# Reordering the first chunk of a fused mLSTM cell and feed-forward block by hand

## The chip, the core and the metric

The kernel runs on one core of a Trainium2 chip. The metric is the device time of one execution in microseconds (us), as the median of several executions. The core has five engines with an instruction queue each, in order: TensorE (PE in the profile, with its weight loads PEld), VectorE (DVE), ScalarE (ACT), GpSimd (POOL) and SyncE (SP, which here only issues DMAs).

## The reference

The first half is an mLSTM cell over 4 batches, 8 heads, 768 tokens and 40 dimensions per head: a decaying outer-product state that each token updates and reads. The second half is a feed-forward block over the 3072 resulting rows of 320 values.

```python
for t in range(S):
    m_new = np.maximum(f_gate[:, :, t] + m, i_gate[:, :, t])
    f_stab = np.exp(f_gate[:, :, t] + m - m_new)
    i_stab = np.exp(i_gate[:, :, t] - m_new)
    C = f_stab[...] * C + i_stab[...] * np.einsum('bhd,bhe->bhde', vt, kt)
    n = f_stab[...] * n + i_stab[...] * kt
    h_tilde = np.einsum('bhde,bhe->bhd', C, qt)
    denom = np.maximum(np.abs(np.einsum('bhd,bhd->bh', n, qt)[:, :, None]), 1.0)
    y[:, :, t] = sigmoid(o_gate[:, :, t]) * h_tilde / denom
...
h = x @ w_in                      # 3072x320 by 320x2048
out = np.maximum(0.01 * h, h) @ w_out
```

## The kernel before

**Tiling.** The 768 tokens are cut into 6 chunks of 128. In each chunk there is one step per batch, so steps 0 to 3 are chunk 0, steps 4 to 7 chunk 1, and so on. A cell step turns 128 tokens of 8 heads into one block of x, and the four blocks of a chunk, transposed, are the 512 columns (`xT`) of the feed-forward block for that chunk. The feed-forward block of chunk c runs on TensorE between the cell steps of chunk c+1.

**Chunk 0** is the subject here. It has no earlier state, so a step works on plain scores:

- `gates` (scans on VectorE, L293 to L312) and `gates_exp` (ScalarE, L318 to L324) make the decay factors. `gates_T` (called by `u_gates(1)` for chunk 1) transposes them with TensorE (L341, L346) and copies them out with VectorE (L354, L356).
- `spread_first` builds the decay exponents of two steps in four PSUM banks with TensorE (L460 to L477); `first_exp` (ScalarE, L488) takes their exponential into the weights `w`.
- `u_transpose` transposes k and q of a step (TensorE L598, tile `tkq`), and a copy (L601, on VectorE for step 0, on ScalarE for the others) gives `kqT`.
- `u_scores` multiplies them (TensorE L610), and VectorE multiplies the scores into `w` (L614).
- `u_natural` transposes k back (TensorE L620, ScalarE copy L622); `prep_vu` scales v for the state (POOL, L513 and L517); `u_state` multiplies both (TensorE L631, `dC`) and copies the state (ScalarE L639).
- `u_values` multiplies `w` by v (TensorE L700, `pa`) and makes the reciprocal denominators (VectorE L692 to L694). `prep_o` takes the tanh of the output gate (ScalarE L539); `gate` joins them (VectorE L709, then POOL L713, tile `x`).
- `u_x` transposes a block of x (TensorE L801 and L802), and five ScalarE copies (L804 to L808) put it into `xT`.
- `prepare_tiles` (POOL L153 to L156) and `prepare_step` (POOL L160 to L162) set constant parts of the tiles that the later chunks use. `prepare_step` overwrites parts of the same tile that holds v of the step.

**The weights** come as 64-bit floats. `load_weights(n)` loads a part; `narrow_weights(n)` is a generator of seven passes over it that make 32-bit floats: one on ScalarE (L254) and six on VectorE (L256, L260, L264, L266, L268, L270). In chunk 0 parts 0 and 1 of `w_in` are narrowed, in chunk 1 all the rest, while VectorE also serves the cell.

**Feed-forward units of chunk 0.** `ff_units(0)` gives units of 10 matmuls of 256 columns (L819), each with two ScalarE activations (L827). `ffs[0]` and `ffs[1]` use part 0 of `w_in` and the columns of steps 0 and 1; they run in chunk 0's own code. The others run in the loop over chunk 1, which starts with the split transposes of step 4 (`u_split`, L579, tile `tk`).

**What sets the order.** TensorE, VectorE, ScalarE and POOL run in the order in which `first_chunk` (L1144) calls these functions (`manual_schedule`, L1229). SP's DMAs are placed by a scheduler. PSUM tiles of tag "c" share four buffers, so a new tile waits until an older one has been read. Each DMA that SP issues waits for the one eight places before it to land.

Of the kernel before, what the change touches and what calls it, by code (L numbers as in the profile page):

```python
# [19 lines left out]
def kernel(  # L20
# [110 lines left out]
    for n in range(NL):  # L131
# [2 lines left out]
        nc.gpsimd.memset(S_t[n][:, 1, :, D:], 2.0)  # L134
        nc.gpsimd.memset(S_t[n][SL:, 0], 0.0)

    def mixed(s):

        n = s % 2
        return qn[:, 2 * n : 2 * n + 2]  # L140
# [9 lines left out]
    def prepare_tiles():  # L150

        for u in range(2):
            nc.gpsimd.tensor_copy(cm2[ts(u, SL)], cmask[ts(u, SL), ts(u, SL)])  # L153
        nc.gpsimd.memset(xb[:], 0.0)
        for t in rb_t:
            nc.gpsimd.memset(t[:, :, RL:], 0.0)  # L156

    def prepare_step(n):

# [48 lines left out]
    def load_weights(n):  # L208

        m = n - QN  # L210
        if n < QN:
            dst = w_in[:, n, :]
        else:
            dst = w_out[:, 2 * m : 2 * m + 2, :].rearrange("p a d -> p (a d)")
        to = dst
        if wide:
            if n < 2:
                at = NF * GT - 2 * WC * (n + 1)
                raw = acts_l[:, at : at + 2 * WC].bitcast(U64)
            elif n < QN:  # L220
                raw = raw_t[:, WC * (n - 2) : WC * (n - 1)]
            elif m < 2:
                raw = w_out[:].rearrange("p f d -> p (f d)")[:, (2 + m) * WC : (3 + m) * WC].bitcast(U64)
            else:
                at = (4, 0, 1, 2, 3, 4)[m - 2] * HW
                raw = raw_t[:, at : at + HW]
            raws[n] = (raw, dst)
            to = raw
        if n < QN:
            src = moe_w_in[:, n * QC : (n + 1) * QC].rearrange("(k p) (r c) -> r p k c", p=DP, r=2)  # L230
            at = [0, 0]
            for r in (0, 1, 0, 1):
                k0, m = run_of(r, at[r])
                nc.sync.dma_start(
                    to[DP * r : DP * (r + 1), 2 * P * at[r] : 2 * P * (at[r] + m)].rearrange("p (k c) -> p k c", k=m),
                    src[r, :, k0 : k0 + 2 * m - 1 : 2, :],
                )
                at[r] += m
        else:
            rows = moe_w_out[2 * m * P : 2 * (m + 1) * P, :]  # L240
            nc.sync.dma_start(to.rearrange("p (a d) -> p a d", d=Dm), rows.rearrange("(a p) d -> p a d", p=P))
# [118 lines left out]
    def load(s):  # L360
        c, b = divmod(s, B)
        rows = ts(c, P)
        d = st.setdefault(s, {})
        n = s % NL
        d.update(k=kn[:, n], q=qn[:, n])
        if c == 0:
            d["va"] = S_t[n][:, 1]
            for t, src in ((kn, k), (qn, q)):
                nc.sync.dma_start(  # L369
                    t[:, n].rearrange("p h d -> p (h d)")[:, : TJ * D], src[b, :, rows, :].rearrange("h (g j) d -> h g (j d)", j=TJ),  # L370
                )
            nc.sync.dma_start(d["va"][:, :, :D], v[b, :, rows, :].rearrange("h p d -> p h d"))
            return
        if s not in asked:
            load_kq(s)
        for u in range(2):
            for i in range(2):
                nc.sync.dma_start(
                    S_v[n][ts(u, SL), u, :, i, :DB],
                    v[b, :, c * P + u * SL : c * P + (u + 1) * SL, DB * i : DB * (i + 1)].rearrange("h p d -> p h d"),  # L380
                )
# [11 lines left out]
    def load_o(s):  # L393
        c, b = divmod(s, B)
        at = NF * GT - 4 * WC - (s + 1) * Dm
        st.setdefault(s, {})["o"] = acts_l[:, at : at + Dm]
        nc.sync.dma_start(
            st[s]["o"].rearrange("p (h d) -> p h d", d=D), o_gate[b, :, ts(c, P), :].rearrange("h p d -> p h d"),
        )
# [54 lines left out]
    def spread_first(a, s2):  # L454


        M = H // RG
        ab = [psf.tile([P, 2, M, P], F32, name=f"ab{r}", tag="mm") for r in range(RG)]
        for r in range(RG):
            nc.tensor.matmul(  # L460
                ab[r][:].rearrange("p n m t -> p (n m) t"), lhsT=identb, rhs=cmaskb.unsqueeze(1).to_broadcast([P, 2 * M, P]),
                start=True, stop=False,
            )
        for n in range(2):
            for m in range(M):
                for r in range(RG):
                    bh = (s2 + n) * H + m * RG + r
                    rows = ts(r, BH)
                    nc.tensor.matmul(
                        ab[r][:, n, m, :], lhsT=ident[rows, r * BH + bh : r * BH + bh + 1].to_broadcast([BH, P]),  # L470
                        rhs=a[rows, :], start=False, stop=False,
                    )
        for r in range(RG):
            rows = ts(r, BH)
            at = r * BH + s2 * H + r
            ones = ident[rows, at : at + (2 * M - 1) * RG + 1 : RG]
            nc.tensor.matmul(  # L477
                ab[r][:].rearrange("p n m t -> p (n m) t"), lhsT=i0[rows, :], rhs=ones.unsqueeze(2).to_broadcast([BH, 2 * M, P]),
                start=False, stop=True,
            )  # L480
        return ab

    def first_exp(ab, s2):

        for n in range(2):
            w = st[s2 + n]["w"] = wk.tile([P, H, P], F32, name="w", bufs=NL)
            for r in range(RG):
                nc.scalar.activation(w[:, r::RG, :], ab[r][:, n], AF.Exp)  # L488
# [47 lines left out]
    def prep_o(s):  # L536

        o = st[s]["o"] if s < B else natural(s, 2) if s < 2 * B else raw_blocks(s, 2, DB)
        nc.scalar.activation(o, o, AF.Tanh, scale=0.5)  # L539
# [63 lines left out]
    def u_scores(s):  # L603
        d = st[s]
        kqT, w = d["kqT"], d["w"]
        sc = [psc.tile([P, PR, P], F32, name=f"sc{r}", tag="c") for r in range(2)]
        for j in range(PR):
            for r in range(2):
                rows = slice(DP * r, DP * r + D)
                nc.tensor.matmul(  # L610
                    sc[r][:, j, :], lhsT=kqT[rows, 0, ts(j, P)], rhs=kqT[rows, 1, ts(j, P)], start=True, stop=True,
                )
        for r in range(2):
            nc.vector.tensor_tensor(w[:, r::2, :], w[:, r::2, :], sc[r][:], op=ALU.mult)  # L614
# [71 lines left out]
    def u_state(s):  # L686
        state(s)
        state_copy(s)
# [388 lines left out]
    def u_gates(c):  # L1077
        gates_T(c, bus.pop(c)[0])
# [65 lines left out]
    def first_chunk():  # L1144

        load_fi(1)
        load_fi(2)
        for n in range(2):
            load(n)
        load_weights(0)  # L1150
        load_o(0)
        load_o(1)
        for n in range(2, B):
            load(n)
        load_o(2)
        load_o(3)
        load_weights(1)
        gates(0)
        gates_exp(0)
        bu, a, _ = bus[0]  # L1160
        warm(9)
        ab = spread_first(a, 0)
        gates_T(0, bu)
        first_exp(ab, 0)
        gates(1)
        u_transpose(0, nc.vector.tensor_copy)
        gates_exp(1)
        u_transpose(1, nc.scalar.copy)
        prep_vu(0)
        prep_vu(1)  # L1170
        load_kq(B)
        u_scores(0)
        ab = spread_first(a, 2)
        u_scores(1)
        first_exp(ab, 2)
        u_natural(0)
        u_natural(1)
        w = narrow_weights(0)
        next(w, None)
        u_values(0)  # L1180
        u_values(1)
        next(w, None)
        next(w, None)
        prep_o(0)
        gate(0)
        prep_o(1)
        gate(1)
        prepare_tiles()
        u_x(0)
        u_x(1)  # L1190
        for _ in w:
            pass
        u_transpose(2, nc.scalar.copy)
        u_transpose(3, nc.scalar.copy)
        ffs = ff_units(0)
        ffs[0]()
        u_state(0)
        u_state(1)
        prepare_step(0)
        prepare_step(1)  # L1200
        u_scores(2)
        u_scores(3)
        prep_o(2)
        prep_o(3)
        ffs[1]()
        u_values(2)
        gate(2)
        u_values(3)
        gate(3)
        w = narrow_weights(1)  # L1210
        next(w, None)
        next(w, None)
        u_x(2)
        u_x(3)
        prep_vu(2)
        prep_vu(3)
        for _ in w:
            pass
        u_gates(1)
        u_natural(2)  # L1220
        u_state(2)
        u_natural(3)
        u_state(3)
        prepare_step(2)
        prepare_step(3)
        return ffs
# [125 lines left out]
```

## Time and profile before

| quantity | value |
|---|---|
| median of 3 runs | 510.76 us (510.48 to 511.11) |
| the profiled execution's own time | 510.94 us |
| its span (first to last instruction) | 509.1 us |
| TensorE busy (matmuls) | 495.4 us, 97% of the span |
| TensorE weight loads | 385.9 us, 76% |
| VectorE busy | 332.4 us, 65% |
| ScalarE busy | 179.3 us, 35% |
| POOL busy | 143.2 us, 28% |
| mean DMA rate | 116 GB/s |

A busy TensorE is not TensorE at its peak: the chip grants it a clock, shown as PEclk in tenths of full speed, and a matmul at half clock is busy for longer. The profile also cuts the span into 40 slices of 12.7 us with the busy tenths of each engine; the first five slices (to 63.6 us) hold chunk 0 and the start of chunk 1. A wait is named by what ended it.

### The profile page before, as it was taken

The numbers are of one execution on the slowest core, as the hardware profiler recorded it, in microseconds if no ns is written. First come the engines' busy times: TensorE is split into PE (matmuls) and PEld (weight loads), VectorE is DVE, ScalarE is ACT, GpSimd is POOL, SyncE is SP. The second block draws the span as 40 slices with busy tenths as digits, with TensorE's granted clock in tenths as the row PEclk, the third lists the DMA queues.
The fourth block names the chain that finished last, engine by engine and source line by source line (L and its number), as shares of the span: only waits on it lengthen the run. The fifth ranks groups of instructions, "written<-read, shape, count | busy, mean of one in ns | idle before, by whom it ended". The sixth has DMA issues, their size and how long they took to land.

```text
span 509.1 us, 13257 instructions
## 1 busy us (share of the span) xinstructions
PE 495.4 (97%) x5362; PEld 385.9 (76%) x5362; DVE 332.4 (65%) x543; ACT 179.3 (35%) x476; POOL 143.2 (28%) x177
## 2 busy tenths in 40 slices
PE   8788899999999999999999999999999999999997
PEld 7667688867755469965479965489955489999997
DVE  5455888899963976824976734867633767864831
ACT  4465657752552331042421133511312510035210
POOL 4063905434320501620502701403700302200011
PEclk9878699999999999999999999999999999999999
DMA  6999976597460584872685872775871211200001
GB/s 130 174 175 169 256 135 183 125 203 140 96 159 7 116 160 133 152 152 85 135 161 131 141 161 79 155 149 120 162 186 30 55 53 41 88 4 1 1 1 52
DMA packets 157556, 59.25 MB, mean 116 GB/s; under 512 B 120056, under 2 KB 148280, under 8 KB 157496
## 3 DMA queue, kind: packets, MB, share of 16 engines
q1 hardware_dynamic: 117428, 51.20, 44.7%
q10 hardware_dynamic: 40068, 7.21, 9.2%
q8 instruction: 42, 0.69, 0.6%
q14 instruction: 18, 0.15, 0.1%
HBM read 51.68 MB, written 6.70 MB: 115 GB/s over the span
## 4 chain that ended last, share of the span: by engine, by line
PE 89%; SPq 3%; DMA 3%; DVE 2%; issue 1%; POOL 1%; ACT 1%; ACTq 0%; DVEq 0%; POOLq 0%
PE ph L819 34%; PE po L897 30%; PE pq L1004 6%; PE po L854 6%; PE pT L754 3%; PE sd L673 3%; SPq L369 2%; DMA kn<-in_k_dram 1%; PE tkq L598 1%; PE sd L678 1%; DMA fi<-in_f_gate_dram 1%; PE tk L579 1%; DMA S<-in_v_dram 1%; PE pa L700 1%; POOL x L713 1%
## 5 line engine op out<-in xcount | busy, mean ns | idle before, releaser
L819 PE MATMUL ph<-xT,w_in 64*128 64x512 f32 (+1 forms) x960 | 180.7, 526 | 0.5 <-issue 0.5
L819 PEld LDWEIGHTS ph<-xT,w_in 64*128 64x128 f32 x960 | 92.4, 189 | 74.8 <-issue 68.2
L897 PEld LDWEIGHTS po<-w_out,acts 128*128 128x128 f32 x640 | 87.3, 190 | 3.4 <-issue 3.0
L897 PE MATMUL po<-w_out,acts 128*128 128x160 f32 x640 | 89.1, 300 | 0.0
L827 ACT ACTIVATE acts<-ph 128x512 f32<-128x512 f32 (+1 forms) x96 | 45.5, 522 | 121.7 <-PE ph L819 108.4
L651 POOL TENSOR_TENSOR S<-S,f 40x336 f32<-40x336 f32 x36 | 31.8, 883 | 132.6 <-PE pT L754 94.1
L683 DVE TENSOR_TENSOR qn<-w,sd 64x512 f32<-64x512 f32 x40 | 27.4, 684 | 43.8 <-PE sd L678 28.4
L503 ACT ACTIVATE w<-w,gT 128x64 f32<-128x64 f32 x160 | 41.2, 337 | 21.3 <-DMA S<-in_v_dram 15.8
L897 PE MATMUL po<-raw,acts 128*128 128x160 f32 x320 | 44.7, 300 | 0.0
L897 PEld LDWEIGHTS po<-raw,acts 128*128 128x128 f32 x320 | 43.6, 190 | 0.3
L854 PE MATMUL po<-w_out,acts 128*128 128x320 f32 x128 | 36.5, 436 | 0.0
L495 POOL TENSOR_TENSOR w<-w,i 128x512 f32<-128x512 f32 x20 | 29.0, 1458 | 25.3 <-DMA w<-a_dr 10.5
L768 POOL TENSOR_TENSOR xb<-xb,den 128x320 f32<-128x320 f32 x16 | 11.6, 727 | 76.5 <-DVE xb L765 76.5
L761 DVE STREAM_TRANSPOSE hb<-pT 128x512 f32<-128x512 f32 x16 | 11.4, 713 | 31.0 <-PE pT L754 30.8
L854 PEld LDWEIGHTS po<-w_out,acts 128*128 128x128 f32 x128 | 23.6, 190 | 9.3 <-issue 0.3
L556 DVE TENSOR_TENSOR qn<-kqT,ea 64x512 f32<-64x512 f32 x32 | 27.0, 845 | 1.0
L932 POOL TENSOR_TENSOR y<-y,raw 128x160 f32<-128x160 f32 x10 | 8.2, 819 | 64.9 <-ACT y L931 64.9
L673 PEld LDWEIGHTS sd<-kqT 40*64 40x64 f32 x640 | 19.8, 135 | 6.1 <-issue 6.1
L772 DVE STREAM_TRANSPOSE x<-xb 128x512 f32<-128x512 f32 x16 | 18.0, 1124 | 7.7 <-POOL xb L768 7.7
L897 PE MATMUL po<-raw 128*128 128x160 f32 x160 | 22.6, 299 | 0.0
L897 PEld LDWEIGHTS po<-raw 128*128 128x128 f32 x160 | 22.0, 190 | 0.0
L673 PE MATMUL sd<-kqT 40*64 40x64 f32 x640 | 21.3, 220 | 0.0
(205 smaller groups left out, 701.4 us busy)
## 6 DMA issues: line engine op xcount, KB each, us to landing
rb<-in_k_dram SPq DMA_DIRECT2D x64, 80.0 KB
rb<-in_q_dram SPq DMA_DIRECT2D x64, 80.0 KB
rb<-in_o_gate_dram SPq DMA_DIRECT2D x64, 80.0 KB
ea<-a_dr SPq DMA_DIRECT2D x32, 128.0 KB
raw<-in_moe_w_out_dram SPq DMA_DIRECT2D x6, 640.0 KB
w<-a_dr ACTq DMA_DIRECT2D x24, 128.0 KB
xT<-x_dr SPq DMA_DIRECT2D x32, 96.0 KB
x_dr<-x SPq DMA_DIRECT2D x64, 40.0 KB
```

The source lines that it names most:

```text
L495: nc.gpsimd.tensor_tensor(w, w, cm2.unsqueeze(1).to_broadcast([P, H, SL]), op=ALU.add)
L503: yield nc.scalar.activation(w[:, h, :], w[:, h, :], AF.Exp, bias=gT[c][:, 0, bh : bh + 1], scale=1.0)
L556: nc.vector.tensor_tensor(mixed(s)[rows, 1 - r], d["kqT"][rows, 1].rearrange("p (h t) -> p h t", t=SL), d["ea"][rows], op=ALU.mult,)
L651: nc.gpsimd.tensor_tensor(new, old, g, op=ALU.mult)
L673: nc.tensor.matmul(bank[1 - u][toks, h, :], lhsT=kqT[rows, 0, ts(h, SL)], rhs=kqT[rows, 1, ts(h, SL)], start=True, stop=True,)
L683: nc.vector.tensor_tensor(mixed(s)[toks, u], w[toks], bank[1 - u][toks], op=ALU.mult)
L772: nc.vector.transpose(in_blocks(xq[:]), xb[:].rearrange("p (j n) d -> p j n d", n=TB))
L819: nc.tensor.matmul(ph[r][:, cols], lhsT=w_row(r, slot, j), rhs=xT[DP * r : DP * (r + 1), slot, cols], start=(slot == 0), stop=(slot == KC ...
L827: nc.scalar.activation(acts[:, f, cols], ph[r][:, cols], AF.Prelu, alpha=0.01)
L854: nc.tensor.matmul(po[n][:], lhsT=acts[:, f, ts(n, P)], rhs=w_out[:, f, :], start=(f == 0), stop=(f == NF - 1),)
L897: nc.tensor.matmul(bank[:], lhsT=left[:, f, :], rhs=right[:, f, :], start=f == 0, stop=f == KH - 1)
L1004: nc.tensor.matmul(bank[r][:, e, :], lhsT=left(r)[rows, e], rhs=right(r)[rows], start=n == 0, stop=n == len(terms) - 1,)
```

## The change

Only `first_chunk`, the place of one group of memsets and the order of some loads change. No instruction is added or removed.

```diff
+    for t in rb_t:
+        nc.gpsimd.memset(t[:, :, RL:], 0.0)
...
         nc.gpsimd.memset(xb[:], 0.0)
-        for t in rb_t:
-            nc.gpsimd.memset(t[:, :, RL:], 0.0)
...
+        load_weights(1)
         load_o(2)
         load_o(3)
-        load_weights(1)
...
         u_scores(0)
+        u_scores(1)
         ab = spread_first(a, 2)
-        u_scores(1)
         first_exp(ab, 2)
+        u_gates(1)
         u_natural(0)
         u_natural(1)
-        w = narrow_weights(0)
-        next(w, None)
         u_values(0)
         u_values(1)
-        next(w, None)
-        next(w, None)
+        prepare_tiles()
+        prepare_step(0)
+        prepare_step(1)
+        w = narrow_weights(0)
+        for _ in range(3):
+            next(w, None)
         prep_o(0)
+        prep_o(1)
         gate(0)
-        prep_o(1)
         gate(1)
-        prepare_tiles()
+        u_transpose(2, nc.scalar.copy)
+        u_state(0)
+        u_transpose(3, nc.scalar.copy)
+        u_state(1)
         u_x(0)
         u_x(1)
+        prep_vu(2)
+        prep_vu(3)
         for _ in w:
             pass
-        u_transpose(2, nc.scalar.copy)
-        u_transpose(3, nc.scalar.copy)
         ffs = ff_units(0)
         ffs[0]()
-        u_state(0)
-        u_state(1)
-        prepare_step(0)
-        prepare_step(1)
         u_scores(2)
         u_scores(3)
         prep_o(2)
         prep_o(3)
-        ffs[1]()
         u_values(2)
-        gate(2)
         u_values(3)
-        gate(3)
         w = narrow_weights(1)
         next(w, None)
-        next(w, None)
+        ffs[1]()
+        gate(2)
+        gate(3)
         u_x(2)
         u_x(3)
-        prep_vu(2)
-        prep_vu(3)
         for _ in w:
             pass
-        u_gates(1)
         u_natural(2)
```

In words, engine by engine. **TensorE**: the scores of step 1 stand before the second `spread_first`; the gate transposes of chunk 1 move from behind the last x up to just behind that `spread_first`; the transposes of steps 2 and 3, with the state products of steps 0 and 1 between them, stand before the x transposes of steps 0 and 1 instead of behind them and behind `ffs[0]`; the values of steps 2 and 3 stand before `ffs[1]` instead of behind it. **ScalarE**: the copies of those tiles move likewise, so four `kqT` copies and two state copies come before the ten `xT` copies of steps 0 and 1; the first pass of `narrow_weights(1)` comes before the activations of `ffs[1]`. **VectorE**: the two gate copies move up; both denominators of steps 2 and 3 come before both gate products. **POOL**: the constant memsets and copies come before the products of x(0) and x(1), and the scaled v of steps 2 and 3 before the products of x(2) and x(3). **SP**: part 1 of `w_in` is asked for before the output gates of steps 2 and 3; a few loads for chunk 1 change places with neighbours.

## The prediction, made before the result was known

> **What bounds the kernel now.** I read the slices first, for where TensorE is not full and what clock it has.
>
> ```profile
> PE   8788899999999999999999999999999999999997
> ...
> PEclk9878699999999999999999999999999999999999
> ```
>
> Only the first five slices (63.6 us) have room: from there on TensorE is full at full clock, and the 448.6 us behind 60.4 hold 444.4 us of it. So the change is worth what it moves the start of the chunk 1 loop, unless the loop gives it back. Second, the chain of waits in order of time, for what fills those 60 us (start, length, what):
>
> ```profile
> 25.27 0.49 DVE x L709
> ...
> 26.51 1.98 POOL x L713
> ...
> 29.43 5.52 PE tkq L598 x128
> 34.95 2.36 PE ph L819 x20
> ...
> 42.85 3.71 PE pa L700 x32
> ...
> 47.76 1.18 POOL x L713
> ...
> 52.27 0.43 ACT kn L622
> ...
> 54.72 0.43 ACT kn L622
> ```
>
> After each pair of `pa`, TensorE waits for gate products on VectorE and POOL; the `tkq` of steps 2 and 3 stand behind that wait, and the end of the chunk is a ping-pong between TensorE and ScalarE copies. Third, stretches of 2 us, for the granted clock (columns: length, busy time of PE, PEld, DVE, ACT, POOL, then PEclk, DMA share, GB/s):
>
> ```profile
> 22.00:24.00 2.00, 1.16 (x10) 1.01 (x9) 0.73 (x4) 0.06 (x1) 0.00 (x0) 0.69 0.94 179
> 24.00:26.00 2.00, 0.00 (x0) 0.00 (x0) 1.97 (x4) 0.00 (x0) 0.17 (x1) 0.50 1.01 138
> ...
> 32.00:34.00 2.00, 2.00 (x58) 2.00 (x57) 0.21 (x1) 1.41 (x2) 1.77 (x5) 0.75 1.17 199
> 34.00:36.00 2.00, 2.00 (x44) 1.84 (x40) 0.00 (x0) 2.00 (x3) 0.02 (x1) 1.00 1.46 140
> ...
> 46.00:48.00 2.00, 1.36 (x8) 0.87 (x7) 1.51 (x6) 0.00 (x0) 0.96 (x2) 0.67 1.41 154
> ...
> 60.00:62.00 2.00, 2.00 (x20) 1.71 (x20) 1.97 (x2) 1.76 (x6) 1.92 (x3) 0.92 1.05 358
> ```
>
> Only 1.0 and 0.5 stand in undivided stretches, so the mixed means place the switches: down at about 22.8, up at 33.0, down at 46.7, up at 60.3. The distances (10.2, 13.7, 13.6) are 3, 4 and 4 times 3.41 us. Each fall comes at the end of 3.8 us of `pa`, during which PE was busy without a gap; each rise after several us of dense `tkq` or `ph`. At half clock a tile of 16 `tkq` matmuls takes 1.70 us instead of 1.05, and a `ph` unit about 4.3 instead of 2.4.
>
> [...] The sum goes by the trace.
>
> **The change, part by part**, on the trace's clock; the sum counts to the ScalarE pass L254 of `w_in` part 2, at 56.80, which opens the work of the loop (its `kqT` copies and exponentials follow without a gap).
>
> *To the end of the first values.* Scores of step 1 before `spread_first`: both are 1.1 and 3.2 us on either side, so the exchange is free; the exponentials of steps 2 and 3 slip from 17.13 to about 18.2 and the copies L622 and L254 behind them end near 22.8 instead of 21.3, still ahead of the second denominators, at 24.5, that L256 stands behind. The gate transposes took 0.46 + 0.85 at half clock, so about 0.65 at full, now in front of `pa`. `pa` ends at 23.16 + 0.65 = **23.8**, and L709 moves from 25.27 to 25.9.
>
> *The stretch to `ffs[0]`, now ScalarE's.* x is ready at 27.3 and 29.2, as before plus 0.65, but TensorE goes on with `tkq` at 23.8. ScalarE then has, in this order: four `kqT` copies (3.04 for three, so 4.05), two state copies (1.25 for four, so 1.25 for both steps), ten `xT` copies (27.54 to 29.21, 1.67 a step, 3.34). They sum to 8.64. They start after the first `tkq` tile, at 24.9. One stall comes between: the k tile of step 3 waits for the PSUM buffer of step 2's q copy and takes 1.05, of which the state copy covers 0.62, so about 0.5. `ffs[0]` starts at 24.9 + 8.64 + 0.5 = **34.05** against 34.88: **-0.83**. VectorE's narrowing ended at 32.2; plus 0.65, plus 0.4 because POOL now scales v beside it (L268 took 1.89 beside POOL's L513 and L517, 1.49 otherwise), it ends at 33.3. It is late next, by 0.75.
>
> *The clock under `ffs[0]`.* Before, TensorE reached it straight from dense `tkq`, at full clock. Now it runs dry from about 30.8 (second x transpose) to 34.05. With the switch points of before it falls at 33.0 and rises at 36.4, and of the 2.36 us at half clock half is lost: **+1.2**. The bounds are 0 (no fall) and +2.4 (no rise before 39.8).
>
> *From `ffs[0]` to the last `xT` copy.* Before it took 51.59 - 34.88 = 16.71. Now: `ffs[0]` 2.43, scores of step 2 1.07, the product L614 and its start 1.33 (step 3's pair lies under `pa`), `pa` 2 x 1.89, together 8.61; then `ffs[1]` 2.36 runs while VectorE and POOL make x (denominator 0.57, L709 0.45, L713 0.72, so 1.74: hidden); then activations 0.74 and ten `xT` copies 3.34. Sum 15.05: **-1.66**. If `ffs[1]` falls to half clock behind `pa`, up to 1.9 of it is lost.
>
> *From there to L254.* Before 5.21, with the gate transposes, the first `nk` on TensorE and 1.02 us for POOL's memsets (L161) in it. These are gone: v of steps 2 and 3 is scaled on POOL near 29 to 35, so the memsets end before 50. Left, at half clock: copy 0.43, `dC` 0.79, `nk` 1.06, copy 0.43, `dC` 0.79, state copies 0.62, hand-overs 0.25, together 4.37: **-0.84**. At full clock it would be 3.1, so -2.1.
>
> *Edits that cost nothing.* POOL idles from 13.6 to 25.8 before, so the constants fit there. Only the two copies L153 have no clean row: they took 2.36 beside VectorE; the nearest rows are L517, 0.23 alone and 1.47 contended; two take 0.5 to 2.9 us, and I take 0.5, VectorE being mostly idle at 18.4, when `spread_first` frees their tile. `prepare_step(1)` waits for `pa` until 23.8 and ends at 24.9, an us ahead of x. The rb memsets (0.46 together) fill POOL's idle time at 5.6. On SP, `w_in` part 1 is asked for from 21.45 instead of 25.64, and gets no use of it: L254 reads it at 43.2 before, at about 39 now. The two o loads move from 21.45 to about 24.3 and take 4.1 us to issue; the DMA engines are saturated there (share 1.0). Nearest row for the delay: the v load of 20.95, 3.92 us to its waiter; I allow up to three times that, so o lands between 32 and 40. The tanh is due at about 38, so the cost lies between 0 and 2; I take 0, nearest to the row. SP's later v loads of steps 4 and 5 wait for the memsets of `prepare_step`, now ten us earlier, so they come no later.
>
> *The loop.* VectorE is 93% busy in it and its idle times are its only reserve. But its first pass there waited 2.05 us for L254 itself, so it moves with it, and I take no loss.
>
> **Sum**: -0.83 + 1.2 - 1.66 - 0.84 = **-2.1 us** against the profiled execution's 510.94, so 508.8; its median is 0.18 lower, so I forecast **508.6**.
>
> **The rivals.**
>
> *The clock holds (chance 0.20).* Short matmuls in the pause may keep the clock at 1.0 up to `ffs[0]`; then +1.2 goes, and the tail is 3.1: -0.83 - 1.66 - 2.1 = -4.6, **506.2**. For it: `tkq` and `dC` lie denser before the pause than anything did at 25. Against it: the clock fell in a busy `pa`.
>
> *The clock is lost twice, and the kernel is slower (0.19).* `pa` lets it fall at 22.8 as before; `tkq` of step 2 then starts cold, ScalarE starts 0.65 later and stalls 0.3 longer, so `ffs[0]` starts at 35.0 (+0.1) and leaves the next window only 1.4 us of dense work. The clock stays down to 39.8, so +2.4. `pa` of steps 2 and 3 then ends near 46, and `ffs[1]`, now behind it, falls cold too, before it had run ahead of it at full clock: +1.7. Sum 0.1 + 2.4 - 1.66 + 1.7 - 0.84 = +1.7, **512.3**. It decides when `ffs[0]` starts later than about 34.7. For it: all four switch points of before are kept; against it: before, 3.4 us of cold `tkq` were enough to raise it at 33.0.
>
> *Nothing is left (0.21).* One cold unit costs its upper bound, or VectorE in the loop gives the lead back: there TensorE waited for VectorE's L735 (0.7 us) at 111. Then +-0.8, about **510.6**. For it: 93% busy; against it: the 2.05 us at the loop's start.
>
> **The numbers.** The likeliest case has 0.40 and by itself spans 507.6 to 509.7. The range takes in the full clock of the first rival and the loss of the second, 505.8 to 512.4. About 0.2% (1 us) is what a measurement here can tell from no change. Faster by more than that: 0.20 plus nearly all of 0.40, 0.57. Within: 0.21 plus a rest, 0.24. Slower: 0.19.
>
> **What would show it.** Right, if ScalarE runs from 24.9 to 34 with less than 1 us idle, `ffs[0]` starts near 34, no wait of TensorE for POOL's x stands ahead of the third x transpose, `ffs[1]` lies under the gate products, and L254 of part 2 starts near 54.7. The clock rows at 33, 36.4, 46.7 and 60 decide between the rivals. Wrong, if ScalarE waits for a DMA before the tanh of step 2, if `ffs[0]` waits for VectorE's L270, or if the loop's start is early and the end is not.

## The result and the profile after

The changed kernel takes **513.0 us** (median of 20 runs, 508.68 to 515.79); the kernel before, on the same chip, 510.35 us (509.07 to 511.54). The ratio is 1.0045, with a 95% interval of 1.0025 to 1.0066: it is slower by 2.65 us between the medians, where 508.6 was forecast. The profiled execution is the longest of the 20, 515.79 us with a span of 514.0, so its stretches are the effect at its largest. A second and a third execution of the same kernel were profiled later, at 509.18 and 511.19 us; the three together show what spreads.

The slices of the page (busy tenths and granted clock of TensorE, 12.9 us each):

```profile
PE   8959799999999999999999999999999999999997
...
PEclk9976799999999999999999999999999999999999
```

Against the page of before, TensorE's second slice is fuller (9 for 7), its third emptier (5 for 8), and the fourth is full, but at 6 tenths of the clock where it had 8. Behind the fifth no digit has changed: the 453.6 us behind 60.4 hold 448.8 us of TensorE's work, where the 448.6 of before held 444.4. So the loss was made before the loop, and it is read there. First what TensorE waited for between 22 and 62 us (engine, line, what it waited for: us in total, times, longest), in the kernel before and then in the changed one:

```profile
PE xt L801 <- POOL x L713: 6.0, 4, 3.4
PE dC L631 <- ACT kn L622: 1.2, 2, 0.6
```

```profile
PE xt L802 <- POOL vu L518: 4.4, 1, 4.4
PE dC L632 <- ACT kn L623: 3.2, 1, 3.2
PE ph L820 <- ACT xT L805: 1.5, 1, 1.5
PE tkq L599 <- ACT kqT L602: 0.9, 1, 0.9
```

The four waits for x are gone, as the change intends. In their place stands one wait of 4.4 us at the transpose of x, and it is put down to something that has nothing to do with it: L518 scales v for a later step. The timeline of the changed kernel shows the place (start, length, engine, line, what; in brackets the idle time ahead):

```profile
29.36 1.15 PE L599 MATMUL tkq<-ident,kn 128*64 128x64 f32 x32 [0.89 <-ACT kqT L602]
...
31.27 0.48 PE L632 MATMUL dC<-vu,rb 128*40 128x42 f32 x16
36.19 0.69 PE L802 MATMUL xt<-ident,x 128*128 128x128 f32 x2 [4.44 <-POOL vu L518]
```

And GpSimd's own timeline in the same stretch:

```profile
27.72 2.65 POOL L714 TENSOR_TENSOR x<-x,den 128x320 f32<-128x320 f32 x2 [2.09 <-DVE x L710]
...
35.05 0.22 POOL L518 TENSOR_TENSOR vu<-S,gT 128x16 f32<-128x16 f32 x1
```

Both x were ready at 30.4, TensorE was done with the work ahead of them at 31.75, and the transpose began at 36.19. No engine's result was missing.

What was missing were TensorE's own **instructions**. They arrive by DMA, in a queue of their own, and the page lists that queue: `q8 instruction: 42` packets with 0.69 MB, that is 16 KB each; for TensorE's 10,858 recorded instructions (5362 matmuls, 5362 weight loads and 134 semaphore waits and drains) that makes about 258 a packet. That this queue is TensorE's is inferred from this count and from what follows.

When a packet moved is found by narrowing the window of the DMA view. From 26.5 to 33.0 us only data moved (queue, packets, MB, share of 16 engines):

```profile
## 3 DMA queue, kind: packets, MB, share of 16 engines
q1 hardware_dynamic: 1504, 1.19, 116.5%
```

and from 33.0 to 34.6 the packet is there:

```profile
q1 hardware_dynamic: 491, 0.12, 79.1%
q8 instruction: 1, 0.02, 5.9%
```

With TensorE's recorded instructions numbered from 0, the pauses of the table below, which no wait explains, stand at the numbers 449, 961, 1473 and 1729, that is 449 + 256n: those are taken as the **edges** of the blocks. From the records of the traces (us; a pause is counted from the start of the last instruction ahead of the edge to the start of the first behind it):

```
kernel, edge        block ahead   next packet       first instr.   pause   packet end
                    entered       from - to         behind edge            to first
before, 961         31.24         35.38 - 36.49     37.90          0.36    1.41
before, 1473        52.98         60.81 - 61.90     63.33          0.92    1.43
before, 1729        63.33         66.26 - 67.84     69.20          0.38    1.36
changed, 449        10.22         13.83 - 15.15     16.51          0.98    1.36
changed, 961        26.45         33.06 - 34.58     36.19          4.64    1.61
```

TensorE goes on 1.4 to 1.6 us after the packet's end in all five rows, and in them the next packet sets out 2.9 to 7.8 us after the block ahead has been entered. The records show when a packet moves, not when it is asked for; that it is asked for at the entry is the theory of e1 and no more. The entry is dated by the first instruction that ran, so it can be late where TensorE stands waiting just ahead of it: at edge 1473 of the changed kernel the packet set out at 57.31, and the block ahead was entered at 60.35, in the matmuls that had waited 3.2 us for the keys' copy. The kernel before has these pauses too, of 0.4 to 0.9 us, of which TensorE idled 0.0 to 0.5. In the changed kernel `tkq` and `dC` of steps 2 and 3, some 320 short instructions, come straight behind `pa`; the block is through 5.1 us after it was entered, while the packet set out only 6.6 us after. The edge, 961, falls between the last `dC` and the first transpose of x.

The rest of the loss is the clock. Here are the stretches from the end of `pa` to the end of ffs[1] (stretch: length, busy time and instructions of PE, PEld, DVE, ACT, POOL, then PEclk, DMA share, GB/s):

```profile
24.75:31.75 7.00, 6.11 (x160) 5.87 (x160) 6.79 (x10) 3.98 (x6) 4.80 (x6) 0.78 1.16 176
31.75:36.19 4.44, 0.00 (x0) 0.00 (x1) 2.73 (x2) 1.52 (x3) 3.52 (x3) 0.82 0.85 102
36.19:39.25 3.06, 1.54 (x6) 1.05 (x7) 0.00 (x0) 2.03 (x7) 0.00 (x0) 0.50 0.89 133
39.25:46.11 6.86, 6.86 (x52) 5.87 (x52) 0.79 (x2) 3.42 (x9) 0.00 (x0) 0.59 0.94 184
46.11:55.83 9.72, 9.58 (x55) 8.42 (x54) 5.95 (x14) 0.47 (x1) 2.73 (x3) 0.65 0.89 140
```

In the last two TensorE has hardly a gap and runs at 0.59 and 0.65 of its clock. The units in them, from the timeline:

```profile
39.25 4.64 PE L820 MATMUL ph<-xT,w_in 64*128 64x256 f32 x20 [1.52 <-ACT xT L805]
...
46.11 5.75 PE L701 MATMUL pa<-S,w 128*128 128x41 f32 x32
51.80 4.03 PE L820 MATMUL ph<-xT,w_in 64*128 64x256 f32 x20
...
60.28 0.51 PE L632 MATMUL dC<-vu,kn 128*40 128x42 f32 x16 [3.21 <-ACT kn L623]
```

Before, ffs[0] took 2.43 us and `pa` 3.77, both at full clock. The changed order has its own measure of a full clock in e1 below: there `pa` takes 4.09 us at a granted clock of 1.00 (0.3 of it is a wait for VectorE's product L615), and ffs[1] 2.43.

```profile
41.28 4.09 PE L701 MATMUL pa<-S,w 128*128 128x41 f32 x32
45.30 2.43 PE L820 MATMUL ph<-xT,w_in 64*128 64x256 f32 x20
```

**Where the time went.** L255 of part 2 (L254 before), to which the prediction counted, moved from 56.80 to 63.54, by 6.7 us:

- ffs[0] starts at 39.25 instead of 34.88: +4.4;
- ffs[0], `pa` and ffs[1] at a lower clock, against 2.43, 4.09 and 2.43 at full clock: 2.21 + 1.66 + 1.60 = +5.5;
- from ffs[0] to the last `xT` copy, without that clock: 20.53 - 5.47 = 15.06 instead of 16.71, so -1.65;
- from there to L255 3.76 instead of 5.21: -1.45.

The loop gives 1.8 us of this back (span +4.9). In the execution of 509.18 us the same four terms are -0.2, +2.2, -1.9 and -1.5, together -1.4. So behind the start of ffs[0] the new order by itself gains 3.1 to 3.4 us in both, and what varies, and takes the gain away, is the stop and the clock.

### The profile page after: what moved, and what is told of

Same layout as the page of the kernel before. It is cut to its first block, busy times and chain, and to the rows that moved or that the text cites. A ratio compares the mean times of both kernels' runs of the same rounds, so it can differ in the third digit from the quotient of the medians.

```text
span 514.0 us, 13259 instructions
## 1 busy us (share of the span) xinstructions
PE 496.3 (97%) x5362; PEld 387.8 (75%) x5362; DVE 332.4 (65%) x543; ACT 179.4 (35%) x476; POOL 143.2 (28%) x177
## 4 chain that ended last, share of the span: by engine, by line
PE 84%; ACT 4%; DVE 3%; SPq 3%; DMA 3%; issue 1%; POOL 1%; ACTq 0%; POOLq 0%
PE ph L820 32%; PE po L898 30%; PE pq L1005 6%; PE po L855 6%; PE pT L755 3%; PE sd L674 3%; SPq L370 2%; DMA acts<-in_moe_w_in_dram 1%; PE pa L701 1%; DMA fi<-in_i_gate_dram 1%; PE sd L679 1%; ACT w L504 1%; ACT kqT L586 1%; POOL vu L514 1%; ACT acts L828 1%
## 5 line engine op out<-in xcount | busy, mean ns | idle before, releaser
L820 PEld LDWEIGHTS ph<-xT,w_in 64*128 64x128 f32 x960 | 93.6, 193 | 76.4 <-issue 68.0
```

The lines of the kernel that those rows point to most:

```text
L820: nc.tensor.matmul(ph[r][:, cols], lhsT=w_row(r, slot, j), rhs=xT[DP * r : DP * (r + 1), slot, cols], start=(slot == 0), stop=(slot == KC ...
```

## The experiments

Each was run beside the kernel before on the same chip, whose medians there were 510.46 (e1 to e4), 510.62 (e5 to e8), 510.69 (e9 to e12) and 510.82 us (e13, e14). "Wait" is the time from the entry of the block of edge 961 to the start of the packet, from the records; "stop" is TensorE's idle time at that edge.

**e1, the changed kernel again.** No edit.

> The changed kernel, unaltered, once more. Theory (instruction fetch): TensorE's instructions come in packets of 16 KB (256 instructions), the next one asked for when the one before is entered; behind the weight and gate loads the packet is late, and TensorE, now fed quickly, runs dry just ahead of the transpose of x (L802). Expected: again a stop of 2 to 5 us there though x is ready by 30.5, ended 1.3 to 1.7 us after an instruction packet's end; ffs[0] (L820) starts at 37 to 39.5; 510.5 to 516 us. Rival (a real dependency, GpSimd's scaled v, L518, as the profile infers): the stop ends where L518 ends, whatever the packets do. Rival (clock window alone): the stop is an accident and is not seen again, and the time follows only the granted clock.

513.68 us (507.32 to 515.33), ratio 1.0041 (1.0009 to 1.0073): the result repeats. In the profiled execution, 509.18 us, the packet came from 29.19 to 30.47 (wait 5.0) and the transpose of x began at 31.95, 1.48 later; ffs[0] started at 34.65, earlier than expected, since here the stop is only 3.0 us. GpSimd's L518 ends at 31.6, so the rival is not ruled out by this run, but by e2.

**e2, the loads as before.**

```diff
-        load_weights(1)
         load_o(2)
         load_o(3)
+        load_weights(1)
```

> The changed kernel with the loads as before (o of steps 2 and 3 ahead of part 1 of w_in); all else stays. Fetch theory: the same backlog stands ahead of the same packet, only in another order, so the stop ahead of x's transpose stays, 1.5 to 4.5 us long; 510.5 to 514 us. Rival (the load order is the loss): the stop goes, ffs[0] starts by 35, and the time falls to 507.5 to 509.

510.7 us, ratio 0.9995 (0.9978 to 1.0011). Here the theory was right and my expectation from it wrong: the stop went, because the wait was only 2.3 us. Among the small packets of o (570 of the 571 packets below are under 512 B) the packet waited 2.3 us; behind part 1 of `w_in` it waited 5.5 us with o out of the way (e3), and 2.3 us with part 1 moved back (e13). The DMA view from 26.2 to 27.4 us, and TensorE's timeline:

```profile
q1 hardware_dynamic: 570, 0.09, 46.6%
q8 instruction: 1, 0.02, 5.6%
```

```profile
28.89 0.44 PE L802 MATMUL xt<-ident,x 128*128 128x128 f32 x2 [0.20 <-POOL x L714]
...
32.97 4.64 PE L820 MATMUL ph<-xT,w_in 64*128 64x256 f32 x20 [3.20 <-DVE w_in L271]
```

x is transposed at 28.89, while GpSimd's L518 ran at 29.91 and 33.36: it never was a condition. Now ffs[0] waits for VectorE's narrowing, 1.9 us earlier than in the kernel before, and runs cold.

**e3, o later still.**

```diff
         load_weights(1)
-        load_o(2)
-        load_o(3)
...
         load_kq(B)
+        load_o(2)
+        load_o(3)
```

> The changed kernel with the loads of o for steps 2 and 3 issued later, behind the k and q loads of step 4, so that some 6 us of small packets are gone from the backlog ahead of 33 us. Fetch theory: the packet comes by 31.5, the stop ahead of x's transpose shrinks to under 2 us, ffs[0] starts at 34 to 36.5; 507.5 to 510.5 us. Rival (clock alone, or the reordered work itself): the stop or the time stays, 511.5 to 514.

513.84 us, ratio 1.0058 (1.0035 to 1.0081); wait 5.5 us, stop 3.45 us. The expectation missed: with o out of the way the packet comes no sooner. This, with e2, is what points to part 1.

**e4, eight throw-away matmuls fewer.**

```diff
-        warm(9)
+        warm(1)
```

> The changed kernel with 1 instead of 9 of the throw-away matmuls near 5 us, that is 16 instructions fewer (a weight load and a matmul each) and nothing else. Fetch theory: the block's edge falls 16 instructions later in the program, behind the 14 of x's two transposes: they run as soon as x is there (by 31.5), and TensorE stops inside the first instructions of ffs[0] instead, until the packet has landed; ffs[0] has its bulk at 36 to 36.5 instead of 39.25, and the time falls by 1.5 to 3 us to 509.5 to 511.5. All rivals (dependency on L518, loads, clock): 16 instructions at 5 us change nothing at 31 us; xt still at about 36, time within 1 us of the changed kernel's.

511.52 us, ratio 0.9998 (0.9971 to 1.0025). The profiled execution has the packet as late as the profiled one of the changed kernel (33.11 to 34.66, wait 6.6), and yet:

```profile
30.66 0.44 PE L802 MATMUL xt<-ident,x 128*128 128x128 f32 x2
...
35.00 4.64 PE L820 MATMUL ph<-xT,w_in 64*128 64x256 f32 x20 [3.46 <-DVE w_in L271]
```

The eight matmuls are 32 recorded instructions, not the 16 that the expectation counted: in the trace each is two weight loads and two matmuls (the nine of the changed kernel stand as x18), and 10,826 are recorded instead of 10,858. So the edge now lies 32 instructions later, 19 into ffs[0] and behind x's transposes, which run at once: 32 instructions before 6 us moved a wait at 31 us. Only the fetch theory expected that. One detail missed: there is no stop inside ffs[0], since the narrowing held it until 35.0 and the edge was reached at 36.45, when the block was there.

**e5, x ahead of the transposes of steps 2 and 3.**

```diff
-        u_transpose(2, nc.scalar.copy)
-        u_state(0)
-        u_transpose(3, nc.scalar.copy)
-        u_state(1)
         u_x(0)
         u_x(1)
+        u_transpose(2, nc.scalar.copy)
+        u_state(0)
+        u_transpose(3, nc.scalar.copy)
+        u_state(1)
```

> The changed kernel with the transposes of steps 2 and 3 (and the two states) back behind x; loads and the rest as changed. Fetch theory: the two transposes of x lie before the block's edge again and no longer wait for it; the edge then lies near the end of the transposes, whose next packet has more time to come; ffs[0] starts at 35 to 37 and the time is 509.5 to 511.5. Rival (the second pass is the loss, not the stop): 512.5 to 514.5, as with the whole change.

511.32 us, ratio 1.0016 (0.9994 to 1.0038). The stop moves to the new place of the edge, in the middle of 16 equal matmuls, and now the profile finds no releaser at all and calls it "issue":

```profile
34.89 0.39 PE L632 MATMUL dC<-vu,rb 128*40 128x42 f32 x10
37.66 0.35 PE L632 MATMUL dC<-vu,rb 128*40 128x42 f32 x6 [2.37 <-issue]
```

The packet came from 35.07 to 36.10; 1.56 us later TensorE went on. ffs[0] started at 37.93, later than expected, but at full clock (2.43 us).

**e6, the load order alone on the kernel before.** The edit of e2 the other way round.

> The kernel before with one part of the change, the loads of o for steps 2 and 3 behind part 1 of w_in. Fetch theory: in the old order TensorE enters the block at 31 and needs the next one only after 37, when part 1 has passed, so the load order alone costs little: 509.5 to 511.5, no stop over 1 us at a block's edge. Rival (the load order is a loss by itself, through GpSimd's or ScalarE's waits for o or SP's stop): 512 to 514.

510.23 us, ratio 0.9999 (0.9983 to 1.0015), no pause at the edge: the block is entered at 31.47 and through at 38.18, and the packet was there at 36.3. By itself this part of the change costs nothing.

**e7, the second pass alone on the kernel before.**

```diff
         prep_o(2)
         prep_o(3)
-        ffs[1]()
         u_values(2)
-        gate(2)
         u_values(3)
-        gate(3)
         w = narrow_weights(1)
         next(w, None)
-        next(w, None)
+        ffs[1]()
+        gate(2)
+        gate(3)
```

> The kernel before with one part of the change, the second pass: the values of steps 2 and 3 ahead of ffs[1], the gates and part 1's second narrowing step behind it. The forecast's term: the last copy of x to xT comes 1.66 us earlier, 508.5 to 509.2. What the runs so far suggest: the ten copies of xT on ScalarE now all stand behind ffs[1]'s outputs, and the copy of the keys (L622) behind them, so that TensorE waits 2.5 to 3.2 us for it ahead of the state's matmuls where it waited 0.6: the gain is given back, 509.8 to 511.5.

510.79 us, ratio 0.9997 (0.9977 to 1.0017): nothing, where -1.66 was forecast. `pa` took 4.40 and ffs[1] 4.64 us, where 3.77 and 2.43 are those of the full clock in the order before: +2.8 us against the gain of the order, since the clock fell at 43.81. The state's matmuls waited 2.3 us there, put down to GpSimd's memset of S (L160), so the copy of the keys was not what held this one.

**e8, a new order.** Loads as in e2, and then:

```diff
+        u_scores(2)
         ffs = ff_units(0)
         ffs[0]()
-        u_scores(2)
         u_scores(3)
...
         u_values(2)
-        u_values(3)
         w = narrow_weights(1)
         next(w, None)
-        ffs[1]()
+        u_values(3)
+        u_natural(2)
+        u_state(2)
+        u_natural(3)
+        u_state(3)
         gate(2)
         gate(3)
         u_x(2)
         u_x(3)
+        ffs[1]()
...
-        u_natural(2)
-        u_state(2)
-        u_natural(3)
-        u_state(3)
```

> A new order on the changed kernel: loads as before the change; step 2's scores ahead of ffs[0], step 3's behind it; the values of steps 2 and 3, then their natural keys and states, then the transposes of x, and ffs[1] last. If both causes are right (no packet behind part 1 of w_in at the edge ahead of x; the keys' copy not behind the ten copies of xT), TensorE has neither the stop ahead of x nor the wait of 2.5 to 3.2 us ahead of the state, the loop's first transposes come 2 to 5 us earlier than in the kernel before (56.0), and the time is 504.5 to 508.5. If either is wrong: 509 to 513.

**504.98 us** (504.44 to 506.04), ratio 0.9895 (0.9875 to 0.9915): faster than both kernels, and its six runs lie within 1.6 us, where the 20 of the changed one spread over 7. The wait is 1.5 us and there is no stop. The second pass:

```profile
42.80 0.64 PE L621 MATMUL nk<-ident,kqT 128*128 128x128 f32 x4
44.04 0.51 PE L632 MATMUL dC<-vu,kn 128*40 128x42 f32 x16 [0.61 <-ACT kn L623]
44.48 0.66 PE L621 MATMUL nk<-ident,kqT 128*128 128x128 f32 x4
45.80 0.51 PE L632 MATMUL dC<-vu,kn 128*40 128x42 f32 x16 [0.67 <-issue]
46.24 0.44 PE L802 MATMUL xt<-ident,x 128*128 128x128 f32 x2
```

The 0.67 called "issue" stands at no edge: the copy of the keys that these matmuls read ended at 45.71, so this one is a plain wait. The states are done while VectorE and GpSimd make x, ffs[1] covers x's copies, and the loop's first transposes start at 49.40 instead of 56.0.

**e9, e8 with o behind part 1.** The edit of e2 the other way round, on e8.

> The order that took 505.0 us, with the one edit of the change that took no time in the kernel before: the loads of o behind part 1 of w_in. Fetch theory: here, as in the changed kernel, TensorE reaches a block's edge just ahead of x's transposes; the packet stands behind part 1 again, and the stop of 3 to 5 us comes back: 507.5 to 512 us. Rival (the load order costs nothing here either, as alone on the kernel before): 504.5 to 505.5.

509.23 us, ratio 0.9968 (0.9949 to 0.9986), so 4.25 us slower than e8. The stop is back, with the same false name:

```profile
35.66 0.69 PE L802 MATMUL xt<-ident,x 128*128 128x128 f32 x2 [3.90 <-POOL vu L518]
```

The packet ended at 34.25 (wait 6.5), 1.41 us before. An edit that is free in e6 costs 4.25 us here.

**e10, e8 with step 1's state behind x.**

```diff
-        u_state(1)
         u_x(0)
         u_x(1)
+        u_state(1)
```

> The order that took 505.0 us, with step 1's state (dC matmuls on TensorE, two copies of 0.3 us on ScalarE) behind x's transposes: x's first copy starts 0.6 us earlier, ffs[0] starts at 33.2 to 33.8 instead of 34.31. If the window from 30.9 to 34.3 now counts as busy, ffs[0] runs at the full clock, 2.43 instead of 4.07 us; 502.5 to 504.5 us. If not, 504 to 505.2.

505.24 us, ratio 0.9881 (0.986 to 0.9902), no better than e8. ffs[0] started at 34.87, not earlier: the scores of step 2, ahead of it, now waited 1.02 us for x's last copy, presumably for a PSUM buffer that it had to free. Its clock was not spared either (3.86 us).

**e11, e2 with the natural keys and states ahead.** Only the second half of e8's edit; the scores stay.

> The changed kernel with the loads as before the change, and in the second pass the natural keys and the states of steps 2 and 3 ahead of the gates, x's transposes and ffs[1] (the scores stay behind ffs[0]). If the keys' copy behind the ten copies of xT is the second cause, TensorE's wait of 3.2 us ahead of the state shrinks to under 1 us, and the time falls by 2 to 4 us against the 510.7 with the loads alone put back: 506.5 to 508.7. If the second cause is only the half clock of ffs[0] and of the values: 509.5 to 511.

507.66 us, ratio 0.9934 (0.991 to 0.9959): 3.0 us less than e2, on another chip. TensorE's wait for the keys' copy falls from 3.2 to 0.6 us. `pa` and ffs[1] took 4.09 and 2.43 us, where e2's took 5.54 and 4.25, so these 3 us are the two together.

**e12, both undone:** the edits of e2 and e5.

> The changed kernel with both undone: the loads as before and x ahead of the transposes of steps 2 and 3. What is left of the change is the exchange of scores and spread, the constants and the second pass. If the loss comes only from the loads and the transposes together, this is at the time of the kernel before, 509.5 to 511; if the rest has a loss of its own, 511.5 to 514.

511.32 us, ratio 1.0006 (0.999 to 1.0022). No clear loss is left. Its stop, 2.1 us, is the one of e5, since the states still stand ahead of ffs[0].

**e13, part 1 of w_in later.**

```diff
-        load_weights(1)
         load_o(2)
         load_o(3)
...
         load_kq(B)
+        load_weights(1)
```

> The changed kernel with part 1 of w_in loaded later, behind the k and q loads of step 4; the loads of o for steps 2 and 3 stay where they are in the queue otherwise. If it is part 1's packets that the instruction packet stands behind (and not those of o), the packet that TensorE needs at x's transposes starts within 3 us of the block's entry and there is no stop over 1 us ahead of them; ffs[0] at 33 to 35.5. The time: 509 to 511.5, as with the loads as before, unless part 1, now late, holds up its own narrowing (then up to 513). If o's packets are what it stands behind: 5 us or more from entry to packet, and the stop stays.

508.89 us, ratio 0.9973 (0.9951 to 0.9996): with this one line moved the changed kernel is faster than the one before, by 1.9 us between the medians. The DMA view from 25.1 to 28.4 us, with o's small packets moving and the instruction packet among them (27.38 to 28.38, wait 2.3), and the transpose of x:

```profile
q1 hardware_dynamic: 2777, 0.48, 101.5%
q8 instruction: 1, 0.02, 1.9%
```

```profile
30.50 0.44 PE L802 MATMUL xt<-ident,x 128*128 128x128 f32 x2
```

The share of the DMA engines is nearly that of the changed kernel (101.5% against 116.5%), and the wait is 2.3 us against 6.6. So what held the packet in these two is, for the most part, not how full they are but which packets are ahead of it. In e2 and e13 part 1, in packets of 2 KB, moves some us later, and there it is the next packet, for edge 1217, that waits: its blocks were entered at 28.89 and 30.50, and it set out at 36.63 and 37.03, after 7.7 and 6.5 us. It did no harm, since TensorE reached that edge only at 54.2 and 52.8.

**e14, the changed kernel once more.** No edit, one execution.

> The changed kernel once more, one look. Fetch theory: the packet starts 5 us or more after the block's entry, TensorE stops ahead of x's transposes and goes on 1.3 to 1.7 us after the packet's end; the later the packet, the longer the time, between 507 and 516 us.

511.19 us. Packet from 31.34 to 32.70 (wait 6.3), transpose of x at 34.31. The three executions of the changed kernel, from the records:

```
time     packet end   stop   ffs[0]          pa     ffs[1]   loop's first transposes
509.18   30.47        3.0    34.65 (4.64)    4.09   2.43     54.6
511.19   32.70        3.8    37.37 (3.93)    4.09   4.12     57.9
515.79   34.58        4.4    39.25 (4.64)    5.75   4.03     62.7
```

In these three, the later the packet, the later all that follows, and the more of it at half clock. But e2 and e4 lost as much to the clock without the stop, so the stop is not its only cause.

## Why the prediction was wrong

**The step that failed** is "They sum to 8.64" with "about 0.5" of stall, up to "`ffs[0]` starts at 24.9 + 8.64 + 0.5 = 34.05". ScalarE did start as said (24.42 in e1) and its `kqT` and state copies ended at 30.50 as said (24.9 + 4.05 + 1.25 + 0.5 = 30.7). Then it idled 2.03 us in e1 and 3.83 in the profiled execution, for transposes that TensorE had no instructions for. The sum held TensorE ready whenever its data were, and the prediction's list of what is late next (the narrowing) left the instruction queue out, though the profile's page lists it. The trace of before showed pauses of 0.36 to 0.92 us at three edges; read as what they are, they would have been a warning: packing 320 instructions behind `pa` reaches the edge 6 us earlier, and that block's packet had set out 4.1 us after the entry even before. Where the packet is there (e2), ffs[0] starts at 32.97, better than forecast.

**"Asked for from 21.45 instead of 25.64, and gets no use of it"**, the cost of o behind `w_in`, 0 to 2 with 0 taken. For the tanh that was right, and alone (e6) it costs nothing. Together with the transposes ahead of x it costs 2.3 to 4.3 us, by another way: 513.0 and 513.7 against e2's 510.7, and e9 against e8, on two chips. Two edits that were priced apart act on one another.

**The clock, "+1.2" with the bounds 0 and +2.4**, is the second step that failed, and in the profiled execution the larger: +5.5 in all, +2.2 in e1, and +5.5 in e2 and e4, where there is no stop at x. Under ffs[0] alone it was +2.2 in these four, near the upper bound; the rest fell on `pa` and ffs[1]. The sum kept the switch points of before (a fall at 33.0, a rise at 36.4); the clock rows of e1 have the fall at 32.92 and the rise only at 39.74, those of the profiled execution 34.60 and 44.84. Where ffs[0] follows dense matmuls, as before and in e5 to e7 and e12, it takes 2.43; in the eleven profiles with x behind the transposes 3.7 to 4.64. So the pause that the order brings goes with a cold ffs[0], whether it is the stop or the wait for the narrowing. That running dry lowers the clock was an estimate of the author's, which the trace of before did not show: its two falls (22.77 and 46.66) came in or just behind a busy `pa`. No run of the changed kernel shows the +1.2: its three executions lost 2.2, 1.5 and 2.2 us under ffs[0] (e9, in another order, 1.2). The falls at 32.92 and 34.60 did come after about 3 us without a matmul (28.94 to 31.95 in e1, 31.75 to 34.60 in the profiled execution). In e10, where the longest idle time of TensorE ahead of ffs[0] is 1.02 us, it still took 3.86.

**"-1.66"** from ffs[0] to the last copy: the order itself gave -1.65 and -1.9, as forecast. The condition that stood beside it, "if `ffs[1]` falls to half clock behind `pa`, up to 1.9 of it is lost", came true in the profiled execution and in e2, e4, e7 and e14 among others, and `pa` lost up to 1.7 as well, which was not foreseen.

**"-0.84"** to L254: -1.45, between the sizes given for half clock (-0.84) and full clock (-2.1). GpSimd's constants, taken at 0.5 for the two copies, and the exchange of scores and spread were not run alone; e12, which has them beside the second pass, has no clear loss.

**The rivals.** "The clock is lost twice" comes nearest with 512.3 (by its own sum of +1.7 on 510.76 it should have been 512.5), and its condition, ffs[0] later than about 34.7, was met in the two slower executions. Its reason, a cold `tkq` of step 2, holds for the profiled execution (3.4 us, against 2.1 in e1) but not for e1, and its price for the clock (+2.4 and +1.7) was not far below what was lost. That 1.4 us of dense work would not raise the clock was an estimate too; in e1 ffs[0] had run for 1.7 us at 36.33, 3.41 us behind the fall, and the clock stayed down to 39.74. But the rival's ffs[0] at 35.0 had no room for the stop of 4.4 us, and no rival had that. "If ffs[0] waits for VectorE's L270" came true in e2 and e4.

**Settled in part:** why the clock falls at the end of a busy `pa` in some executions and not in others. In the clock rows of all 16 traces the switches lie whole multiples of 3.41 us apart, but the phase differs from one execution to the next (the first fall is at 22.77 before and at 24.36 in the profiled execution). So each trace can be divided into its windows of 3.41 us. In twelve windows at full clock `pa` took 3.17 us or more, and the clock was down behind all twelve; in six it took 3.04 to 3.13, and the clock was down behind four. A `pa` of 3.7 to 4.1 us takes that much of a window only if the two nearly begin together, so in these traces the fall goes with where the windows lie. What else lowers the clock stays open: behind some windows with less of `pa` it was down too, though TensorE was busy for about 3.3 us or more of them (2.0 to 2.3 us of `pa` in the profiled execution, e2 and e4, 2.95 in e7). Nor do the runs show at which point of the DMA engines the packet waits; only that at edge 961 it set out after 2.3 us among o's packets (e2, e13) and after 5.0 to 6.6 us behind part 1's.

## What to carry to other kernels

A pause of an engine that has its data, that no releaser explains or that is put down to an unrelated instruction, is worth holding against the engine's numbered instructions (here TensorE's pauses stood at 449 + 256n) and against the packets of its instruction queue: here, in a dense stretch of short matmuls, a block was through in 5.1 us, and its next packet set out 6.6 us after the entry, behind a large weight load. Move the load, and test it by shifting the edge with a few instructions far ahead. In e8 and e11 it paid to put copies that unblock the next matmuls (the natural keys) ahead of copies that only something later reads (x's ten), and a unit whose data are long there (ffs[1]) where it covers such copies.

## What the runs showed of the hardware

- TensorE's instruction packets are 16 KB (42 with 0.69 MB in the changed kernel's profile); the transfer itself took 0.9 to 1.6 us, and where TensorE was stopped, work went on 1.36 to 1.61 us after its end. At edge 961 the start came 0.5 to 2.3 us after the block's entry when part 1 of `w_in` was not ahead of it (e2, e8, e10, e11, e13), and 5.0 to 6.6 us when it was (the changed kernel, e3, e4, e9). In the order of before, where the block is entered near 31, it came 2.7 to 4.2 us after (the kernel before, e5, e6, e7, e12).
- Thirty-two recorded instructions fewer before 6 us moved a stop of 3 to 4.4 us away from x at 31 us (e4).
- The switches of TensorE's granted clock lie whole multiples of 3.41 us apart (16 traces), and it fell behind each of the twelve full-clock windows in which `pa` took 3.17 us or more, though TensorE had hardly a gap in them.
- The profile's releaser can be wrong when no semaphore was missing: "POOL vu L518" stood beside this stop in the changed kernel, e1, e3, e9 and e14, and "issue" in e5 and e12.
